# Two held-back products and a fixed start order in a chunked delta-rule attention feeding two gated layers

## Chip, core and metric

One core of one Trainium2 chip runs the whole program. The metric is the device time of one execution in microseconds (us), the median over several executions. The engines are TensorE (PE; PEld is its weight load), VectorE (DVE), ScalarE (ACT), GpSimd (POOL) and SyncE (SP), which issues the DMAs here.

## What is computed

```python
# attention, per batch b and head h (4 x 8), 768 steps, head size 48
k_n = k / (norm(k) + 1e-6)
for t in range(768):
    y[t] = q[t] @ state
    state = state + beta[t] * outer(k_n[t], v[t] - k_n[t] @ state)
x = y as [3072, 384]
# first layer, width 1536
x = (silu(x @ w_gate) * (x @ w_val)) @ w_out
# second layer, width 2048
x = elu(x @ w_in) @ w_out2
```

q, k, v and beta are float32. The weights arrive as float64, and the kernel turns each into a high and a low float32 part itself.

## The kernel before

The 3072 tokens are cut into 12 groups (NB) of 256, two batches by 128 steps each. For each group there is an attention part and a first-layer part; the second layer (512 tokens at a time, L506 to L538) runs behind all groups and the change doesn't touch it.

Attention of a group: `stage1` normalises k (`norm`, with a Sqrt on ACT), transposes q and k (`trans`, PE), and takes their products (`gram`, PE at L210). `inversion` then inverts a triangular matrix on DVE: four transposes (L227), some 116 small multiplies and adds (L248, L255) that each need the one before, and a transpose back (L263); ACT spreads the result into `zt` (L270). `xstep` (L281) applies it, `gstep` (L294, four rounds over four PSUM banks, copied out by ACT at L298 and completed by DVE at L299) builds the matrices of a step of 32, `chain` (L312) carries the state through them, `yall` (L325) gives y and `xtr` (L340) its transpose, split into `xh` and `xl`.

First layer of a group, for f = 0 to 11: `gv1` (L445) makes the gate and value products, 18 matmuls into one of two PSUM banks; ACT takes the Silu (L466), DVE multiplies (L467), ACT and DVE split the result into two parts of `hb` (L345, L348). `out1` (L479) multiplies `hb` with wo, 9 matmuls that add up in `acc` over all f; after f = 11 ACT copies `acc` out (L486) and SP stores it. `out1` comes LAG = 2 gate products behind its `gv1`. At the end of a group `moe1` empties the list `held`:

```python
while held:
    put(1, held.pop(0), 1.0, out1)
```

While the first layer of group g runs, attention of group g + 1 and the inversion for group g + 2 are merged into the same queues. `merge` orders the pieces by their weights, and each engine runs its queue in order.

Before the first gate product the 18 weight tiles must be loaded (SP, L363 and L366) and decoded in five pieces each: `low` (ACT, L389), `p0` (ACT, L396), `p1` (DVE, L404), `p2` (DVE, L409), and `p3`, a cast on ACT (L345) with a subtraction on POOL (L348). 16 tiles are loaded at the start, the last two when their room is free. Before, `anchor` and `pinned` only bind decode pieces behind the attention work that was emitted last on DVE and ACT, and a scheduler places the rest.

Of the kernel before, what the change touches and what calls it, by code (L numbers as in the profile page):

```python
# [21 lines left out]
def delta_moe_kernel(ctx: ExitStack, tc: tile.TileContext, q, k, v, beta,  # L22
# [9 lines left out]
    nc = tc.nc  # L32
# [30 lines left out]
    NTB = 2  # L63

# [40 lines left out]
    def emit_consts():  # L105
        make_identity(nc, ident)
        V.memset(neg1, -1.0)
# [13 lines left out]

    def emit_zero():
        V.memset(kp[:, :, D:64], 0.0)
        V.memset(qp[:, :, D:64], 0.0)
        G.memset(zt, 0.0)
        G.memset(st[0:32], 0.0)

        for r0, r1 in ((32, 64), (64, 96)):
            for x, n in ((st, B * H), (sv, 2 * (C - 1) * H)):
                w_ = x[r0:r1].rearrange("p b (h d) -> p b h d", d=D) if x is st else \  # L130
                    x[r0:r1].rearrange("p a c (h d) -> p (a c) h d", d=D)
                A.copy(out=w_.rearrange("p b h d -> p (b h) d"),
                       in_=ident[r0:r1, D:2 * D].unsqueeze(1).to_broadcast([32, n, D]))
# [61 lines left out]
    def trans(a, which):  # L195
# [23 lines left out]
    def inversion():  # L219
# [47 lines left out]
        def spread(r):  # L267
            def f():
                q0 = slice(32 * r, 32 * r + 32)
                A.copy(out=zt[q0, :, 32 * (r % 2):32 * (r % 2) + 32],  # L270
                       in_=ain[q0, 0:512].rearrange("p (u i) -> p u i", u=16))
# [4 lines left out]
    def xstep():  # L276
        for n in range(4):
# [6 lines left out]
            A.copy(out=R[:, 4 * n:4 * n + 4, :], in_=p)  # L284

    def gstep(a, par):
        b = 64 * par
        lc = buf['lc', a][par]
        ps_ = [nxt(atb, "at") for c in range(C)]
# [6 lines left out]
        for c in range(C):  # L296
            pv = ps_[c][0:96, 0:320].rearrange("p (s w) -> p s w", s=4)
            A.copy(out=lc[:, :, c, :], in_=pv)  # L298
# [22 lines left out]
    def yall(g, a):  # L321
# [7 lines left out]
        buf['y', a] = TT(f"y{a}", [128, DM])  # L329
        A.copy(out=buf['y', a], in_=p[:, 0:DM])  # L330
# [5 lines left out]
    def xtr(g, a):  # L336
        xs = slice(a * 128, a * 128 + 128)
        p = nxt(atb, "at")[:, 0:DM].rearrange("p (k t) -> p k t", k=KD)
        for kk in range(KD):
            nc.tensor.transpose(p[:, kk, :], buf['y', a][:, kk * 128:kk * 128 + 128], ident)  # L340
# [34 lines left out]
    def decode(n, tmps):  # L375
# [25 lines left out]
        def p1():  # L401
            if bits:
                by = buf[n].bitcast(U8).rearrange("p a (n b) -> p a n b", b=8)
                V.tensor_scalar(out=by[:, :, :, 3], in0=by[:, :, :, 7], scalar1=128, scalar2=None,  # L404
                                op0=ALU.bitwise_and)
# [67 lines left out]
    def out1(g, f):  # L473
# [9 lines left out]
        if f == F1 - 1:  # L483
            for d0, d1 in ((0, 2), (2, KD)):
                t = TT(f"hb{hb_slot()}", [128, d1 - d0, TB])
                A.copy(out=t, in_=acc[:, d0 // 2, 0:(d1 - d0) * TB].rearrange(  # L486
                    "p (d t) -> p d t", t=TB))
                nc.sync.dma_start(out=x2d[g, :, d0:d1, :], in_=t)
# [37 lines left out]
    def out2(n, f):  # L526
# [6 lines left out]
        if f == F2 - 1:  # L533
            for t in range(4):
                o = TT(("xh1", "xl1", "y0", "y1")[next(os2) % 4], [128, DM])
# [5 lines left out]
    def stage1(g):  # L541
        return [(0.4, lambda: (load_v(g, 0), load_v(g, 1), norm(g), nkn(g, 0), nkn(g, 1))),
                (1.0, lambda: (trans(0, 0), trans(1, 0))),
                (1.0, lambda: (kb(g, 0), kb(g, 1), trans(0, 1), trans(1, 1))),
# [9 lines left out]
    def attention(g, nx):  # L554
# [9 lines left out]
        s.append((2.9, xstep))  # L564
        s += [(1.3, lambda a=a, par=par: gstep(a, par)) for a in range(2) for par in range(2)]
# [13 lines left out]
        inv = inversion()  # L579
# [31 lines left out]
    def moe1(g, before, after):  # L611
# [16 lines left out]
        while held:  # L628
# [48 lines left out]
    ABS = 4  # L677
    PRE0 = 3

    def emit_all():  # L680
        load_k(0)
        emit_consts()
        emit_beta()
        load_q(0)
        for n in range(6):
# [3 lines left out]
        first = stage1(0)  # L689
        body, tail = attention(0, 1)  # L690
        for n in range(6, NW - 2):
            first.insert(1 + n - 6, (0, lambda n=n: load_w(n, src1(n))))
        inv = inversion()
        buf['dt'] = TT("dt", [128, 2, 2, DM], I32)
        dec = [decoding(n, ("xh1", 0, "xl1", 1)) for n in range(NW)]
        dec = [pinned(l) for l in dec]
        run(merge(anchor(first), sum(dec[:PRE0], [])))
        load_q(1)
        inv[0] = pinned([(0, inv[0])])[0][1]
        early = []  # L700
        for n in range(PRE0, PRE):
            early += dec[n][:2]
            del dec[n][:2]
        for n in range(PRE0, PRE0 + ABS):
            early.append(dec[n].pop(0))
        run(merge(anchor([(0.1, x) for x in inv]), anchor(early)))
        run(merge(anchor(body), sum(dec[PRE0:PRE], [])))
        for n in range(NW - 2, NW):
            load_w(n, src1(n))
        nd = [PRE]  # L710

        def before(n):
            l = []
            k = 0
            while nd[0] < NW and (nd[0] <= n or k < PACE):
                k += 1
                l += dec[nd[0]]
# [70 lines left out]
```

## Time and profile before

| | us |
|---|---|
| median of three executions | 1307.78 (1303.6 to 1320.31) |
| the profiled execution | 1302.85, span 1301.1 |
| PE busy | 1162.0 (89%) |
| DVE busy | 821.8 (63%) |
| ACT busy | 608.6 (47%) |
| POOL busy | 129.9 (10%) |

PE counts as busy from a matmul's start to its modelled end, so waits inside a run of matmuls can hide in it. Engines run their own queues in order; a row's square bracket tells how long the engine was idle before it and what ended that.

### The profile page before, as it was taken

Reading aid. Unit: us, or ns where it says so; the run is one execution under the profiler, and the core shown is the slowest. Engines: PE = TensorE matmul, PEld = TensorE weight load, DVE = VectorE, ACT = ScalarE, POOL = GpSimd, SP = SyncE. Lnnn points to the kernel's source line nnn. Section 1 sums busy time; section 2 is a strip of 40 time slices with the busy share of each in tenths; the row PEclk is TensorE's granted clock in tenths of the full one; section 3 lists DMA queues with packets and bytes.
Section 4 is the critical chain, followed back from the end, with each engine's and each line's share of the span. In section 5 each row is a group of like instructions: output and inputs, shape, how many; then the busy total and the mean of one; then the engine's idle time right before and its main releaser. Section 6 shows DMA issues by size and latency. Waiting matters only on the chain.

```text
span 1301.1 us, 31342 instructions
## 1 busy us (share of the span) xinstructions
PE 1162.0 (89%) x13086; PEld 1078.5 (83%) x13086; DVE 821.8 (63%) x2709; ACT 608.6 (47%) x1181; POOL 129.9 (10%) x106
## 2 busy tenths in 40 slices
PE   2473999898989898989898989989899999999998
PEld 1363889898888898989888989978689899899897
DVE  6799585848484858585848574467964545454443
ACT  7554534343425252535353524457754545454443
POOL 4353100000000000000000000031300000000000
PEclk9866798889999999999999999989999999999999
DMA  9530202020202020202020100373010101000000
GB/s 298 160 81 1 38 14 39 13 39 10 43 2 51 2 50 2 51 2 50 7 46 2 26 11 5 125 251 104 1 49 1 49 1 49 1 33 1 25 1 25
DMA packets 106815, 57.16 MB, mean 44 GB/s; under 512 B 76945, under 2 KB 101521, under 8 KB 106673
## 3 DMA queue, kind: packets, MB, share of 16 engines
q1 hardware_dynamic: 106672, 55.16, 16.7%
q8 instruction: 102, 1.67, 0.5%
q14 instruction: 41, 0.33, 0.1%
HBM read 45.71 MB, written 9.44 MB: 42 GB/s over the span
## 4 chain that ended last, share of the span: by engine, by line
PE 57%; DVE 34%; ACT 4%; issue 3%; DMA 1%; POOL 1%; SPq 0%; DVEq 0%; ACTq 0%; POOLq 0%
PE gv L445 14%; DVE z L255 7%; DVE ain L248 7%; PE acc L531 7%; PE at L531 7%; PE at L514 7%; PE gv L514 7%; PE acc L479 5%; PE at L294 4%; DVE w L404 2%; PE at L281 2%; DVE hb L348 2%; DVE tb L467 2%; DVE ain L227 2%; PE at L312 2%
## 5 line engine op out<-in xcount | busy, mean ns | idle before, releaser
L445 PE MATMUL gv<-xh,w 128*128 128x256 f32 x1728 | 295.9, 295 | 23.6 <-DVE tb L467 22.9
L445 PEld LDWEIGHTS gv<-xh,w 128*128 128x128 f32 x1728 | 248.9, 200 | 29.4 <-DVE tb L467 24.0
L479 PE MATMUL acc<-hb,w 128*128 128x256 f32 x1296 | 194.9, 298 | 37.6 <-ACT hb L345 34.7
L479 PEld LDWEIGHTS acc<-hb,w 128*128 128x128 f32 x1296 | 172.2, 199 | 45.5 <-ACT hb L345 36.7
L445 PE MATMUL gv<-xl,w 128*128 128x256 f32 x864 | 160.6, 295 | 1.5 <-DVE xl L348 1.5
L466 ACT ACTIVATE tb<-gv 128x256 f32<-128x256 f32 x144 | 54.9, 382 | 216.4 <-PE gv L445 216.0
L467 DVE TENSOR_TENSOR tb<-gv,tb 128x256 f32<-128x256 f32 x144 | 60.7, 422 | 127.6 <-ACT tb L466 126.7
L445 PEld LDWEIGHTS gv<-xl,w 128*128 128x128 f32 x864 | 131.7, 202 | 2.9 <-DVE xl L348 1.7
L345 ACT CAST hb<-tb 128x256 fp32r<-128x256 f32 x144 | 58.4, 406 | 146.8 <-DVE tb L467 146.2
L255 DVE TENSOR_TENSOR z<-z,ain 128x60 f32<-128x60 f32 (+32 forms) x696 | 122.5, 214 | 1.3
L248 DVE TENSOR_TENSOR ain<-z,ain 128x60 f32<-128x60 f32 (+32 forms) x696 | 122.3, 207 | 1.2
L348 DVE TENSOR_TENSOR hb<-tb,hb 128x256 fp32r<-128x256 f32 x144 | 76.7, 533 | 42.7 <-ACT hb L345 41.3
L521 DVE SCALAR_TENSOR_TENSOR hb<-at,hb 128x512 f32<-128x512 f32 x48 | 33.2, 691 | 84.5 <-ACT hb L520 84.5
L521 DVE SCALAR_TENSOR_TENSOR hb<-gv,hb 128x512 f32<-128x512 f32 x48 | 33.1, 690 | 80.2 <-ACT hb L520 72.5
L294 PE MATMUL at<-gr,R 32*96 32x80 f32 x1536 | 75.3, 276 | 8.7 <-DVE w L299 4.4
L294 PEld LDWEIGHTS at<-gr,R 32*96 32x96 f32 x1536 | 64.9, 179 | 19.0 <-DVE w L299 4.6
L520 ACT ACTIVATE hb<-hb,neg 128x512 f32<-128x512 f32 x96 | 69.4, 723 | 2.8
L518 ACT ACTIVATE hb<-at 128x512 f32<-128x512 f32 x48 | 28.6, 595 | 87.6 <-PE at L514 87.6
L518 ACT ACTIVATE hb<-gv 128x512 f32<-128x512 f32 x48 | 28.6, 596 | 85.3 <-PE gv L514 85.0
L281 PE MATMUL at<-R,zt 64*64 64x96 f32 x768 | 38.6, 254 | 27.5 <-ACT zt L270 27.4
L519 ACT ACTIVATE hb<-hb 128x512 f32<-128x512 f32 x96 | 60.6, 632 | 2.7
L281 PEld LDWEIGHTS at<-R,zt 64*64 64x64 f32 x768 | 35.8, 140 | 29.7 <-ACT zt L270 28.2
(174 smaller groups left out, 2154.6 us busy)
## 6 DMA issues: line engine op xcount, KB each, us to landing
w<-in_moe_w_out_dram SPq DMA_DIRECT2D x28, 384.0 KB, 6.6
w<-in_moe_w_in_dram SPq DMA_DIRECT2D x16, 384.0 KB, 5.6
kp<-in_k_dram SPq DMA_DIRECT2D x12, 384.0 KB, 5.4
qp<-in_q_dram SPq DMA_DIRECT2D x12, 384.0 KB, 4.3
w<-in_moe_w_gate_dram SPq DMA_DIRECT2D x12, 384.0 KB, 7.8
w<-in_moe_w_val_dram SPq DMA_DIRECT2D x12, 384.0 KB, 8.0
R<-in_v_dram SPq DMA_DIRECT2D x24, 192.0 KB, 2.6
x2d<-hb SPq DMA_DIRECT2D x12, 256.0 KB, 2.1
```

The lines of the kernel that those rows point to most:

```text
L248: V.tensor_tensor(out=t, in0=z[:, l:l + 1, x:y].to_broadcast([128, l, y - x]), in1=an[:, l, 0:l].unsqueeze(2).to_broadcast([128, l, y - x] ...
L255: V.tensor_tensor(out=z[:, 0:l, x:y], in0=z[:, 0:l, x:y], in1=t, op=ALU.add)
L281: nc.tensor.matmul(p[r:r + 64, j], lhsT=zt[r:r + 64, 4 * n + j, :], rhs=R[r:r + 64, 4 * n + j, :], start=True, stop=True, skip_group_check ...
L294: nc.tensor.matmul(ps_[c][0:96, s * 80:s * 80 + 80], lhsT=R[t, u, :], rhs=gr[t, u, 0:80], start=True, stop=True, skip_group_check=True)
L348: (e2 or V).tensor_tensor(out=lo, in0=src, in1=hi.bitcast(F32), op=ALU.subtract)
L445: nc.tensor.matmul(dst, lhsT=wt[:, a_, kk * 128:(kk + 1) * 128], rhs=xx[:, kk, :], start=(n == 0), stop=(n == 3 * KD - 1))
L467: V.tensor_tensor(out=s, in0=p[:, TB:2 * TB], in1=s, op=ALU.mult)
L479: nc.tensor.matmul(o, lhsT=w[:, a_, d * 128:(d + 1) * 128], rhs=hh[:, b_, :], start=(f == 0 and n == 0 and d != 1), stop=(f == F1 - 1 and ...
L514: nc.tensor.matmul(p, lhsT=W[f][:, 0, a_, kk * 128:(kk + 1) * 128], rhs=x2[n][b_][:, kk, :], start=(m == 0), stop=(m == 3 * KD - 1))
L520: A.activation(out=r, in_=r, func=ACTF.Identity, bias=neg1, scale=1.0)
L521: V.scalar_tensor_tensor(out=r, in0=p, scalar=0.0, in1=r, op0=ALU.max, op1=ALU.add)
L531: nc.tensor.matmul(ob4[t], lhsT=hh[:, b_, t * 128:(t + 1) * 128], rhs=w[:, a_, :], start=(f == 0 and m == 0), stop=(f == F2 - 1 and m == 2))
```

## The change

Three things change.

First, `held` is emptied at a group's end only in the last group. The last two wo products of a group (f = 10 and 11) come behind the first two gate products of the next one. The copy of `acc` no longer goes to an `hb` tile but to one tile `y`, which the two halves of the attention's y now share.

Second, everything up to the first gate product is emitted by `inorder`, which binds each piece behind the one before it on DVE, ACT and POOL: attention of group 0 first, then the inversion together with all `low` pieces, then the attention's remainder merged with the decode of nine tiles (NE; before it was 13, PRE). All 16 weight tiles are issued before v. A Sqrt on one element stands first on ACT.

Third, copies change engines: those that fill `st` and `sv` go from ACT to POOL, behind `kb`, as part of `emit_zero2`; and in group 0 alone ten evacuations (two of `kq`, two of `zt`, two of `R`, four of `lc`) go from ACT to DVE. There `gstep` also uses the four banks of `gv` and `acc` in turn with the four `at` banks.

```diff
+    def emit_zero2():
         G.memset(zt, 0.0)
         G.memset(st[0:32], 0.0)
...
-                A.copy(out=w_.rearrange("p b h d -> p (b h) d"),
-                       in_=ident[r0:r1, D:2 * D].unsqueeze(1).to_broadcast([32, n, D]))
+                G.tensor_copy(x[r0:r1], ident[r0:r1, D:2 * D].unsqueeze(1).to_broadcast([32, n, D]))
...
+    def put(out_, p, on_v):
+        (V.tensor_copy if on_v else A.copy)(out=out_, in_=p)
...
-        A.copy(out=kq[:, a, :, which, :], in_=p)
+        put(kq[:, a, :, which, :], p, g == 0 and a)
...
+        if g == 0 and (a + par) % 2 == 0:
+            ps_ = gvb + [acc[:, 0], acc[:, 1]]
+        else:
+            ps_ = [nxt(atb, "at") for c in range(C)]
...
-        while held:
+        while held and g == NB - 1:
             put(1, held.pop(0), 1.0, out1)
...
-        for n in range(6):
+        for n in range(2):
+            load_w(n, src1(n))
+        for n in range(2, NW - 2):
             load_w(n, src1(n))
...
+        norm_, tq, tk, gm = stage1(0)
+        run(inorder([norm_, tq, piece(0, 0), tk, gm, (0, emit_zero2)]))
+        early = [piece(n, i) for n in range(4) for i in (0, 1)][1:]
+        early += [piece(n, 0) for n in range(4, NW - 2)]
+        inv = inversion(0)
+        run(inorder(merge([(0.1, x) for x in inv[:-4]], early)))
...
+        run(inorder([(0, x) for x in inv[-4:]]))
+        run(inorder(merge(body, pre)))
```

Line numbers of the changed kernel run some 3 to 15 higher: L445 is now L460, L479 L494, L281 L287, L294 L303, L227 L233, L263 L269, L404 L419, L409 L424; `put` is L199, for both engines.

PE at the end of a group in the middle of the program, before. The last gate product of the group (f = 11, bank gv_84) is followed by the wo products of f = 9 and 10 and, behind one matmul of the next group, that of f = 11:

```order
L445 MATMUL gv_84<-xh_140_3448,w_59_1047 128x256 x3
L445 MATMUL gv_84<-xl_141_3449,w_59_1047 128x256 x3
L445 MATMUL gv_84<-xh_140_3448,w_59_1047 128x256 x6
L479 MATMUL acc<-hb_182_4637,w_53_926 128x256 x9
L479 MATMUL acc<-hb_184_4694,w_60_1086 128x256 x9
L445 MATMUL gv_83<-xh_172_4379,w_21_203 128x256
L479 MATMUL acc<-hb_186_4749,w_60_1086 128x256 x9
L445 MATMUL gv_83<-xh_172_4379,w_21_203 128x256 x2
```

The same place in the changed kernel:

```order
L460 MATMUL gv_84<-xh_133_3420,w_62_1157 128x256 x3
L494 MATMUL acc<-hb_174_4638,w_55_1035 128x256 x9
L460 MATMUL gv_83<-xh_163_4349,w_26_436 128x256 x3
L460 MATMUL gv_83<-xl_164_4350,w_26_436 128x256 x3
L494 MATMUL acc<-hb_176_4709,w_63_1188 128x256 x9
L287 MATMUL at_87<-R,zt 64x96 x8
L287 MATMUL at_88<-R,zt 64x96 x8
```

A whole gate product of the next group now stands between the wo products of f = 9 and f = 10; the one of f = 11 has moved behind `xstep` and a second gate product. `xstep` stands one gate product earlier than before.

POOL at the start of the program, before (z is the mask of `norm`, later the inversion's tile; w are decoded weights):

```order
L126 MEMSET st 32x1536
L177 TENSOR_TENSOR z_153<-strict,nbt 128x512
L192 TENSOR_TENSOR gr<-kp,nbt 128x8x48 x2
L348 TENSOR_TENSOR w_21_203<-xh_20_189,w_21_203 128x2x384
L348 TENSOR_TENSOR w_22_222<-dt_140,w_22_222 128x2x384
L230 MEMSET z_307 128x512
```

and in the changed kernel:

```order
L180 TENSOR_TENSOR z_177<-strict,nbt 128x512
L195 TENSOR_TENSOR gr<-kp,nbt 128x8x48 x2
L130 MEMSET zt 128x1024
L131 MEMSET st 32x1536
L136 COPY st<-ident 32x1536
L136 COPY sv<-ident 32x2304
L136 COPY st<-ident 32x1536
L136 COPY sv<-ident 32x2304
L236 MEMSET z_286 128x512
```

Two fills and four copies now stand ahead of the MEMSET of z that the inversion starts from, and two subtractions of the decode behind it.

DVE behind the first inversion, before (its last transpose, then decode pieces of tiles 3 to 5, then `gstep`):

```order
L263 STREAM_TRANSPOSE ain<-z_307 128x32x16
L404 TENSOR_SCALAR w_5_116<-w_5_116 128x768
L404 TENSOR_SCALAR w_6_119<-w_6_119 128x768
L409 SCALAR_TENSOR_TENSOR dt_140<-dt_140,w_5_116 128x768
L409 SCALAR_TENSOR_TENSOR xh_26_424<-xh_26_424,w_6_119 128x768
L404 TENSOR_SCALAR w_7_122<-w_7_122 128x768
L299 TENSOR_TENSOR lc_446<-at_87,kq 48x4x32
```

and in the changed kernel:

```order
L269 STREAM_TRANSPOSE ain<-z_286 128x32x16
L199 COPY zt<-ain 32x16x32 x2
L419 TENSOR_SCALAR w_2_108<-w_2_108 128x768
L424 SCALAR_TENSOR_TENSOR xh_20_282<-xh_20_282,w_2_108 128x768
L199 COPY R<-at_88 128x384
L199 COPY R<-at_86 128x384
L419 TENSOR_SCALAR w_3_111<-w_3_111 128x768
L424 SCALAR_TENSOR_TENSOR dt_165<-dt_165,w_3_111 128x768
```

One tile's pieces (tile 0) now stand between the inversion and the first copy of `R`, which needs `xstep` on PE; ahead of the inversion no decode piece is left on DVE, where three of `p1` and three of `p2` stood.

## Rows read from the trace of the kernel before

**Rows 1.** PE's waits, 190 to 880 us: total us, times, longest.
```profile
PE acc L479 <- ACT hb L345: 33.5, 9, 4.1
```
**Rows 2.** Timeline of one group: start, us, engine, line, [idle before, releaser].
```profile
486.14 1.34 PE L479 MATMUL acc<-hb,w 128*128 128x256 f32 x9
487.41 2.22 DVE L227 STREAM_TRANSPOSE ain<-gr 128x256 f32<-128x256 f32 x4
...
500.62 0.52 PE L445 MATMUL gv<-xh,w 128*128 128x256 f32 x3
502.78 1.24 PE L479 MATMUL acc<-hb,w 128*128 128x256 f32 x9
...
509.99 2.66 PE L479 MATMUL acc<-hb,w 128*128 128x256 f32 x18
512.30 1.08 DVE L263 STREAM_TRANSPOSE ain<-z 128x512 f32<-128x512 f32 x1
513.46 1.25 ACT L270 COPY zt<-ain 32x512 f32<-32x512 f32 x2 [2.42 <-DVE ain L263]
516.46 1.47 POOL L166 TENSOR_TENSOR ain<-kp 128x768 f32<-128x768 f32 x1 [1.89 <-ACT zt L270]
516.86 2.41 PE L479 MATMUL acc<-hb,w 128*128 128x256 f32 x9 [4.10 <-ACT hb L345]
518.13 0.94 DVE L167 TENSOR_REDUCE sm<-ain 128x16 f32<-128x768 f32 x1
521.72 1.28 ACT L466 ACT_TABLE_LOAD   x1
523.94 2.86 PE L281 MATMUL at<-R,zt 64*64 64x96 f32 x64
524.86 0.48 ACT L284 COPY R<-at 128x384 f32<-128x384 f32 x1
...
552.09 1.19 DVE L227 STREAM_TRANSPOSE ain<-gr 128x256 f32<-128x256 f32 x2
```
**Rows 3.** Windows: busy us (x) of PE, PEld, DVE, ACT, POOL; granted clock; DMA.
```profile
141.00:156.00 15.00, 15.00 (x153) 13.51 (x153) 6.41 (x21) 9.15 (x21) 1.66 (x2) 0.54 0.19 38
516.00:521.00 5.00, 4.14 (x21) 4.03 (x22) 2.23 (x2) 2.46 (x5) 1.47 (x1) 0.66 0.05 17
```
**Rows 4.** Timeline, end of group 0.
```profile
185.50 1.34 PE L479 MATMUL acc<-hb,w 128*128 128x256 f32 x9 [1.18 <-ACT hb L345]
```
**Rows 5.** Windows over the start, columns as in rows 3 (last: DMA GB/s).
```profile
0.00:46.80 46.80, 7.46 (x150) 6.34 (x150) 36.34 (x150) 33.19 (x39) 15.61 (x21) 1.00 1.06 306
10.00:44.00 34.00, 4.80 (x137) 4.06 (x136) 30.65 (x140) 22.60 (x30) 10.05 (x7) 1.00 1.08 354
46.80:60.00 13.20, 10.79 (x126) 9.86 (x127) 6.15 (x11) 7.29 (x17) 5.60 (x3) 0.85 0.18 27
0.00:132.40 132.40, 58.89 (x864) 53.04 (x865) 112.62 (x356) 76.08 (x113) 52.67 (x40) 0.78 0.48 133
```
**Rows 6.** Timeline of the start, ACT, POOL and DVE.
```profile
3.25 1.37 POOL L126 MEMSET st<- 32x1536 f32 x1
12.83 0.18 DVE L170 TENSOR_SCALAR sm<-sm 128x16 f32<-128x16 f32 x1 [4.91 <-ACT sm L168]
14.89 2.57 POOL L192 TENSOR_TENSOR gr<-kp,nbt 128x384 f32<-128x384 f32 x2 [4.05 <-DVE kp L184]
...
28.13 0.19 DVE L248 TENSOR_TENSOR ain<-z,ain 128x31 f32<-128x31 f32 x1
43.68 1.06 DVE L263 STREAM_TRANSPOSE ain<-z 128x512 f32<-128x512 f32 x1
46.20 1.88 ACT L270 COPY zt<-ain 32x512 f32<-32x512 f32 x3
...
131.24 1.16 DVE L263 STREAM_TRANSPOSE ain<-z 128x512 f32<-128x512 f32 x1
```

**Rows 7.** DVE's groups of instructions, 0 to 132 us: busy us, mean ns, idle before.
```profile
L404 DVE TENSOR_SCALAR w<-w 128x768 uint8<-128x768 uint8 x18 | 24.9, 1418 | 1.1 <-ACT w L389 1.1
```

More of the change, by code (lines that the diff above doesn't have):

```diff
@@ L283, in xstep, with gstep @@
                                      skip_group_check=True)
-            A.copy(out=R[:, 4 * n:4 * n + 4, :], in_=p)
-    def gstep(a, par):
+            put(R[:, 4 * n:4 * n + 4, :], p, g == 0 and n % 2)
+    def gstep(g, a, par):
         b = 64 * par
         lc = buf['lc', a][par]
-        ps_ = [nxt(atb, "at") for c in range(C)]
+        if g == 0 and (a + par) % 2 == 0:
+            ps_ = gvb + [acc[:, 0], acc[:, 1]]
+        else:
+            ps_ = [nxt(atb, "at") for c in range(C)]
         for s in range(4):
@@ L297, in gstep @@
             pv = ps_[c][0:96, 0:320].rearrange("p (s w) -> p s w", s=4)
[L298 removed]
+            put(lc[:, :, c, :], pv, g == 0 and c == 3)
             V.tensor_tensor(out=lc[0:D, :, c, D:80], in0=pv[0:D, :, D:80],
@@ L563, in attention @@
             s.append((0, lambda: load_k(nx)))
-        s.append((2.9, xstep))
-        s += [(1.3, lambda a=a, par=par: gstep(a, par)) for a in range(2) for par in range(2)]
+        s.append((2.9, lambda: xstep(g)))
+        s += [(1.3, lambda a=a, par=par: gstep(g, a, par)) for a in range(2) for par in range(2)]
         def ch(c):
@@ L675, in pinned, with inorder, wrap, f @@
         return [(w, wrap(x)) for w, x in l]
-    ABS = 4
-    PRE0 = 3
+    def inorder(l):
+        def wrap(x):
+            def f():
+                with ExitStack() as es:
+                    for e in (mybir.EngineType.DVE, mybir.EngineType.Activation,
+                              mybir.EngineType.Pool):
+                        if e in last:
+                            es.enter_context(tc.issue_after(last[e]))
+                    n = len(traced())
+                    x()
+                    for i in traced()[n:]:
+                        last[i.engine] = i
+            return f
+        return [(w, wrap(x)) for w, x in l]
+    NE = 9
     def emit_all():
         load_k(0)
+        emit_beta()
         emit_consts()
-        emit_beta()
         load_q(0)
-        for n in range(6):
+        for n in range(2):
+            load_w(n, src1(n))
+        for n in range(2, NW - 2):
             load_w(n, src1(n))
@@ L688, in emit_all, with piece @@
         emit_beta2()
-        first = stage1(0)
-        body, tail = attention(0, 1)
[L691 to L707, printed above, removed]
+        buf['dt'] = TT("dt", [128, 2, 2, DM], I32)
+        tmps = ("xh1", 0, "xl1", 1)
+        dec = [decode(n, tmps) if n < NW - 2 else None for n in range(NW)]
+        def piece(n, i, w=WD):
+            return (w, lambda: dec[n][i]())
+        norm_, tq, tk, gm = stage1(0)
[4 more added lines that the diff above has]
+        run(inorder(merge([(0.1, x) for x in inv[:-4]], early)))
+        load_q(1)
+        body, tail = attention(0, 1)
+        pre = []
+        for n in range(NE):
+            pre += [piece(n, 2), piece(n, 3), piece(n, 4)]
+            if n + 4 < NE + 2:
+                pre.append(piece(n + 4, 1))
+        run(inorder([(0, x) for x in inv[-4:]]))
+        run(inorder(merge(body, pre)))
+        late_ = []
+        for n in range(NE, NW - 2):
+            late_.append([piece(n, i) for i in ((2, 3, 4) if n < NE + 2 else (1, 2, 3, 4))])
         for n in range(NW - 2, NW):
             load_w(n, src1(n))
-        nd = [PRE]
+        nd = [NE]
         def before(n):
```

51 lines of the change are left out of this document (29 added, 22 removed).

## The prediction

> **What bounds the kernel now.** I began with the table of engines: PE is busy 89% of the span, DVE 63%. So I asked PE's waits first, over the stretch of the twelve groups. One line carries nearly all: the wo product waits for the cast of `hb`, 33.5 us in 9 waits [rows 1].
>
> The timeline of one such place shows what is late. DVE ends the inversion's last transpose at 513.4; ACT then makes two spreads of `zt` ahead of the Silu of f = 11, because that is its queue order, then two more, and only then the cast of `hb`. PE stands idle for 4.10 us [rows 2]. The nine matmuls behind the wait take 2.41 us, double pace, and the granted clock from 516 to 521 is 0.66, a mix of the lower and the higher level [rows 3]. So a boundary costs PE 4.1 us of idling and, as 0.34 of 5 us, another 1.7 us of half clock.
>
> The same rows give the loop that sets the period. From L227 at 487.41 to the next L227 at 552.09 are 64.7 us [rows 2]: 26.0 us of inversion on DVE to 513.4, 10.5 us until `xstep` starts at 523.94, and 28.15 us of PE work from there to the next transposes. Only the middle piece holds a wait.
>
> The start is different. DVE's idle time until the end of the second inversion (132.4) is 132.4 - 112.6 = 19.8 us [rows 5]; from 60 us on it is almost never idle, and PE waits for it. There DVE is the bound.
>
> **The boundary, step by step.** PE's order between the end of `gram` and `xstep` grows by one gate product and loses one wo product. Before, PE went from 486.14 to 509.99 without a long wait and had done six gate and six wo products and the attention's pieces [rows 2]. The changed order adds one of each ahead of the next group's first gate product. A gate product takes 502.78 - 500.62 = 2.16 us; a wo product about 1.1 (half of the 2.41 at half clock is 1.2, less a little for the overlap with the next matmul). So PE comes to that gate product at 486.14 + 23.85 + 3.3 = 513.3. It needs the bank of f = 10, whose multiply stands on DVE just behind the last transpose: 513.4 + 0.4 for it = 513.9. A wait of 0.6 us. The gate product ends at 516.1, the wo product of f = 10 at 517.2. By then `zt` is spread (516.4, where POOL's next work starts, rows 2). So `xstep` starts at 517.2 instead of 523.94: 6.7 us earlier [rows 2].
>
> Then three differences until the next transposes. One wo product more: 1.1. A new wait: ACT does the Silu and cast of f = 11, two table loads around the Sqrt (1.28 each), and the Sqrt waits for POOL (1.47) and DVE (0.94) behind the spreads; Silu of the next gate product and four copies of `R` (0.48 each) come to about 523.1 [rows 2], while PE, done with `xstep` (2.86) and a gate product, wants the copies at 522.2. Wait 0.9. On the other side the four `gstep` rounds now each have a full product between them; before, two neighbours stood with four matmuls between, and I credit 0.8 for that. Sum: 28.15 + 1.1 + 0.9 - 0.8 = 29.35, so the next L227 comes at 546.6 and the period is 59.2: **5.5 us per boundary**, if the clock stays up.
>
> Will it? After the 1.18 us wait at the end of group 0 nine matmuls took 1.34 us, full pace [rows 4], so a wait of 0.6 or 0.9 by itself need not drop it. The bounds are 5.5 (no drop) and 5.5 - 2 x 1.7 = 2.1 (a drop at each of the two waits). I take 4.7, nearer to the first because of that row. Nine boundaries have a wait: 9 x 4.7 = 42. The mean wait is 33.5 / 9 = 3.7, not 4.1, so 9 x 0.4 = 3.6 of that was never there to win: **-39 us**. Group 0's end loses its 1.18 us: **-1**.
>
> The copy of `acc` moves between two `gstep` copies on ACT. It must be done before the wo product f = 0 of the next group, behind a whole gate product and a `gstep` round (over 3 us) for two copies of 0.9 us together, so I cost it at nothing; without that cover it would be up to 0.9 per group. The shared `y` tile is stored some 30 us before the attention writes it again: nothing.
>
> **The start, step by step.** The Sqrt is no longer behind ACT's copies: of DVE's wait of 4.91 us [rows 6] some 4.6 go, and `kb` on POOL starts at 10.3 instead of 14.89 and ends at 12.9. But POOL then does two fills (1.37, rows 6, and by its elements 0.9) and four copies of 1536 or 2304 elements, 7,680 in sum, before the MEMSET of z (0.5) that the inversion needs. The trace has no copy on POOL. Lower bound, the fill's 1.37/1536 = 0.89 ns an element: 6.8 us. Upper bound, the two-input multiply's 1.47/768 = 1.91 ns [rows 2]: 14.7 us. One input is nearer to the fill than to two; I take 9. So the inversion starts at 12.9 + 2.3 + 9 + 0.5 = 24.7 (22.5 to 30.4) instead of 28.13, and with the same 16.6 us (28.13 to 44.74, rows 6) ends at 41.3 (39.1 to 47.0).
>
> The Trainium skill, GPSIMD Engine Reference, section "Elementwise — side-by-side cycle accounting", gives POOL about 1.8 cycles of 1.2 GHz an element at best in a software loop. By that the copies would take an estimated 11.5 us and the inversion end at 43.8, which is 2.5 us above my value and still hidden by what follows. No run so far shows such a copy.
>
> It is hidden because `xstep` also needs v, and v is now issued behind all 16 weight tiles. The bytes ahead of it are those that had landed by about 44 us before: 10 to 44 us moved 354 GB/s without a break [rows 5], 12.0 MB after some 1.8 MB, and 16 tiles of 786 KB with k, q, beta and v are 13.9 MB. So v lands at about 44. ACT's spreads stand behind the `low` of the last tile, which lands one v earlier (0.39 MB, 1.1 us), so at 43.8, plus two spreads of 0.63: 45. Before, the fourth spread ended at 48.1 [rows 6]. `xstep` gains 3 us, and loses up to 1 in POOL's slow case (47.0 plus two spreads on DVE is 48.3).
>
> That gain doesn't count, since DVE is the bound and now starves. Of its 36.3 us of work until 46.8 [rows 5] eight decode pieces are part, and six of these move behind `xstep`: 6 x 1.4 [rows 7] = 8.5 us. Four of the ten copies taken over from ACT come in, 2.3 us. So 30.1 us of work by the time when the first copy of `R` can go (45 plus two of four blocks, about 47), and 17 us idle. What is left is the rest of the same 112.6 us plus all ten copies, 4.7 us by ACT's 0.4 to 0.6 each. Idle time behind it was 7.05 us from 46.8 to 60 [rows 5]; now a tile's two pieces, the norm's reduction and the larger choice of PSUM banks fill part of it, and I take 4. Sum: 112.6 + 4.7 + 17 + 4 = 138.3 against 132.4: **+6 us**. Bounds: 0 later idle and no cost of the copies, -3; POOL's slow case and 7 us of idle, +12. What PE has done by the second `xstep` is the same in both orders, so the loss is passed on whole.
>
> **Sum.** 1302.85 (the profiled execution, 5 us below the median of the runs shown) + 6 - 1 - 39 = **1269 us**.
>
> **The rivals.** *The clock falls at the new waits.* Each boundary has two short waits around products of small tiles. For it: 141 to 156 us ran at 0.54 with PE busy throughout [rows 3]. Against: rows 4. Price: 2.1 a boundary, less the 0.4 of above, 15 in all: 1302.85 + 6 - 1 - 15 = 1293.
>
> *DVE doesn't starve at the start, and the boundaries win in full.* For it: much of DVE's time at the start is contended and may shrink. Then 0 for the start and 9 x 5.1 = 46: 1256.
>
> *Slower: `xstep` and `gstep` fall to half clock in every group.* As said, 141 to 156 us, exactly these products, had 0.54 without idling: 15 x 0.46 = 6.9 us lost. If moving `xstep` next to the boundary's waits brings this into nine more groups, 62 us are lost: 1269 + 62 = 1331. It decides from 4.7 us lost a group on. Against: in the group of rows 2 the same products ran at full pace.
>
> *It doesn't do what it says.* The loop through DVE could hold `xstep` where it was: if DVE's 26 us stretch by the 5 us that PE runs ahead, the wait only moves. For it: DVE is busy throughout those 26 us. Against: the same pieces stand there, five multiplies and splits, in both orders. Then only the half clock goes, 9 x 1.7: 1302.85 + 6 - 15 = 1294, as the first rival.
>
> **Chances.** Forecast 0.55 (1258 to 1280); clock or loop 0.25 (1280 to 1297); full gain 0.14 (1246 to 1258); slower 0.06. The range for 8 in 10 runs from 1249 to 1293. Two per cent, about what a measurement of this kernel can tell, is 26 us: faster takes the full gain, nine tenths of the forecast and a little of the third, 0.65; within 2% 0.30; slower 0.05.
>
> **What would show it.** In the changed profile L494's wait for `hb` should be under 5 us in all, the period from L233 to L233 near 59 us, and the granted clock near 1.00 behind the boundaries. At the start the first `xstep` should stand near 45 and the second inversion's end near 138; DVE should be idle some 10 us before the first copy of `R`. It would be wrong if L287 or L460 waits over 2 us a group, or if clock rows near 0.5 follow `xstep`.

## The result, and the profile after the change

| | before | changed |
|---|---|---|
| median of three executions, us | 1307.78 | 1257.83 (1252.91 to 1258.09) |
| ratio, 95% interval | 1 | 0.959 (0.948 to 0.969) |
| profiled execution, us | 1302.85, span 1301.1 | 1258.09, span 1256.3 |

The ratio comes from interleaved executions of both kernels. A longer comparison further down gives 0.963 (0.960 to 0.967). The kernel is faster by 4%, and the time lies inside the range of the prediction, 11 us below its single number. Two terms of the sum were too small, the gain at the boundaries and the loss at the start, and they pulled in opposite directions.

First, PE's waits in the stretch of the groups, the view of [rows 1] (waiting line and releaser: us, times, longest):

```profile
PE gv L460 <- DVE tb L482: 4.3, 2, 3.0
PE gv L460 <- ACT xh L355: 4.0, 1, 4.0
PE acc L494 <- ACT y L501: 1.7, 1, 1.7
PE at L216 <- issue: 1.6, 1, 1.6
```

The wait for the cast of `hb` (33.5 us in nine times before) no longer appears. What is left are single events: one at the end of group 0 (for `xh`), one at 408 us (issue), the others behind the last `xstep`.

The timeline of one boundary, to be held against [rows 2] (start, us, engine, line; the square bracket is the idle time before):

```profile
471.25 2.21 DVE L233 STREAM_TRANSPOSE ain<-gr 128x256 f32<-128x256 f32 x4
...
496.22 1.16 DVE L269 STREAM_TRANSPOSE ain<-z 128x512 f32<-128x512 f32 x1
497.23 0.41 DVE L482 TENSOR_TENSOR tb<-gv,tb 128x256 f32<-128x256 f32 x1
497.47 0.62 ACT L199 COPY zt<-ain 32x512 f32<-32x512 f32 x1 [3.23 <-DVE ain L269]
497.69 0.62 PE L460 MATMUL gv<-xh,w 128*128 128x256 f32 x3
498.42 1.89 ACT L199 COPY zt<-ain 32x512 f32<-32x512 f32 x3
499.95 1.24 PE L494 MATMUL acc<-hb,w 128*128 128x256 f32 x9
501.12 1.12 PE L287 MATMUL at<-R,zt 64*64 64x96 f32 x21
...
529.68 2.21 DVE L233 STREAM_TRANSPOSE ain<-gr 128x256 f32<-128x256 f32 x4
```

The multiply on DVE that frees the bank of f = 10 ends at 497.64, and PE starts the gate product that needs it at 497.69. The last spread ends at 500.31, `xstep` starts at 501.12. PE has work at every moment: it comes to this gate product 0.05 us behind the multiply, and to `xstep` 0.8 us behind the spread.

Then one period, from `xstep` to `xstep`, in windows (busy us and instructions of PE, PEld, DVE, ACT, POOL; granted clock; DMA share, GB/s). The first row is of the kernel before, the second of the changed one:

```profile
523.94:588.68 64.74, 60.14 (x923) 56.92 (x922) 44.09 (x195) 26.63 (x63) 4.70 (x5) 0.97 0.15 27
```
```profile
501.12:559.55 58.43, 58.43 (x923) 55.53 (x923) 42.74 (x194) 26.31 (x63) 4.71 (x6) 1.00 0.17 29
```

The same 923 matmuls. Before, PE idled 4.60 us of the period and worked at 0.97 of its clock, 60.14 x 0.03 = 1.8 us; together 6.4, and the period is shorter by 6.31. Now PE is busy for the whole period at the full 2.4 GHz. So at this boundary, as far as the profile shows it, nothing more is to be had by waiting less.

The start, in windows as in [rows 5], and the timeline of its starving stretch:

```profile
0.00:49.25 49.25, 9.73 (x190) 8.82 (x191) 30.50 (x149) 23.69 (x32) 17.23 (x23) 0.65 1.06 298
0.00:142.60 142.60, 56.23 (x864) 51.36 (x865) 119.57 (x366) 64.58 (x99) 54.51 (x44) 0.66 0.45 123
```
```profile
38.04 1.08 DVE L269 STREAM_TRANSPOSE ain<-z 128x512 f32<-128x512 f32 x1
41.92 0.96 DVE L424 SCALAR_TENSOR_TENSOR xh<-xh,w 128x768 int32<-128x768 int32 x1
44.30 0.90 ACT L399 ACTIVATE w<-w 128x768 int32<-128x768 uint32 x1 [1.43 <-DMA w<-in_moe_w_val_dram]
45.10 1.24 ACT L199 COPY zt<-ain 32x512 f32<-32x512 f32 x2
49.25 0.56 DVE L199 COPY R<-at 128x384 f32<-128x384 f32 x1 [6.37 <-PE at L287]
141.42 1.17 DVE L269 STREAM_TRANSPOSE ain<-z 128x512 f32<-128x512 f32 x1
```

The first inversion ends 5.6 us earlier than before (38.04 against 43.68 in [rows 6]). ACT's spreads stand behind the `low` of the last tile, at 44.30, and DVE has nothing to do from 42.9 to 49.25. The second inversion's last transpose comes at 141.42 instead of 131.24: 10.2 us late.

**Where the time went.** The start of each `xstep` on PE, read from the two timelines, divides the difference of the spans:

| stretch | before, us | changed, us | gain, us |
|---|---|---|---|
| start to second `xstep` | 133.73 | 143.92 | -10.2 |
| second to third | 59.12 | 59.34 | -0.2 |
| third to the last (nine periods) | 592.46 | 536.56 | +55.9 |
| last `xstep` to the end | 515.79 | 516.48 | -0.7 |
| sum (the spans) | 1301.1 | 1256.3 | +44.8 |

The nine periods gave 6.2 each on average; five of them are between 57.9 and 58.5 us. One, from 380 to 443 us, took 62.92: PE idled 2.6 us in it for "issue", a wait that the profile ascribes to no other engine, and lost 1.7 us to half clock. Such a period, of 61.6 to 65.2 us, stands at the same place in the kernels below that share these groups, so it decides nothing between them; what it comes from stays open.

### The profile page after: what moved, and what is told of

The parts are those of the page before. It is cut to its first block, busy times and chain, and to the rows that moved or that the text cites. A ratio compares the mean times of both kernels' runs of the same rounds, so it can differ in the third digit from the quotient of the medians.

```text
span 1256.3 us, 31338 instructions
## 1 busy us (share of the span) xinstructions
PE 1142.3 (91%) x13086; PEld 1061.5 (84%) x13086; DVE 819.1 (65%) x2719; ACT 596.8 (48%) x1167; POOL 131.7 (10%) x110
## 4 chain that ended last, share of the span: by engine, by line
PE 78%; DVE 10%; DMA 4%; issue 3%; ACT 2%; POOL 1%; SPq 1%; DVEq 0%; POOLq 0%; ACTq 0%
PE gv L460 23%; PE acc L494 11%; PE acc L546 7%; PE at L546 7%; PE at L529 7%; PE gv L529 7%; PE at L303 5%; PE at L321 3%; PE at L287 3%; DVE w L419 2%; PE at L206 2%; PE at L334 1%; DVE ain L254 1%; PE at L216 1%; DVE z L261 1%
## 5 line engine op out<-in xcount | busy, mean ns | idle before, releaser
L460 PE MATMUL gv<-xh,w 128*128 128x256 f32 x1728 | 295.1, 294 | 38.0 <-DVE tb L482 32.8
L460 PEld LDWEIGHTS gv<-xh,w 128*128 128x128 f32 x1728 | 245.1, 197 | 43.6 <-DVE tb L482 33.8
L494 PE MATMUL acc<-hb,w 128*128 128x256 f32 x1296 | 185.5, 288 | 2.3 <-ACT y L501 1.7
L494 PEld LDWEIGHTS acc<-hb,w 128*128 128x128 f32 x1296 | 165.9, 192 | 5.9 <-ACT y L501 1.9
L460 PE MATMUL gv<-xl,w 128*128 128x256 f32 x864 | 155.9, 290 | 0.2 <-issue 0.2
L460 PEld LDWEIGHTS gv<-xl,w 128*128 128x128 f32 x864 | 128.8, 198 | 1.9 <-issue 1.6
L254 DVE TENSOR_TENSOR ain<-z,ain 128x60 f32<-128x60 f32 (+32 forms) x696 | 125.8, 212 | 1.6
L355 ACT CAST hb<-tb 128x256 fp32r<-128x256 f32 x144 | 58.5, 407 | 142.8 <-DVE tb L482 142.7
L358 DVE TENSOR_TENSOR hb<-tb,hb 128x256 fp32r<-128x256 f32 x144 | 68.6, 477 | 29.2 <-ACT hb L355 28.9
L303 PE MATMUL at<-gr,R 32*96 32x80 f32 x1472 | 71.4, 264 | 1.2 <-DVE lc L308 1.2
L533 ACT ACTIVATE hb<-at 128x512 f32<-128x512 f32 x48 | 28.7, 597 | 87.4 <-PE at L529 87.4
L303 PEld LDWEIGHTS at<-gr,R 32*96 32x96 f32 x1472 | 58.5, 167 | 13.5 <-DVE lc L308 2.0
L533 ACT ACTIVATE hb<-gv 128x512 f32<-128x512 f32 x48 | 28.7, 597 | 84.8 <-PE gv L529 84.8
L287 PE MATMUL at<-R,zt 64*64 64x96 f32 x768 | 37.2, 251 | 31.4 <-ACT zt L199 31.4
L287 PEld LDWEIGHTS at<-R,zt 64*64 64x64 f32 x768 | 34.7, 137 | 33.3 <-ACT zt L199 31.8
```

The costliest lines, as they stand in the source:

```text
L254: V.tensor_tensor(out=t, in0=z[:, l:l + 1, x:y].to_broadcast([128, l, y - x]), in1=an[:, l, 0:l].unsqueeze(2).to_broadcast([128, l, y - x] ...
L287: nc.tensor.matmul(p[r:r + 64, j], lhsT=zt[r:r + 64, 4 * n + j, :], rhs=R[r:r + 64, 4 * n + j, :], start=True, stop=True, skip_group_check ...
L303: nc.tensor.matmul(ps_[c][0:96, s * 80:s * 80 + 80], lhsT=R[t, u, :], rhs=gr[t, u, 0:80], start=True, stop=True, skip_group_check=True)
L358: (e2 or V).tensor_tensor(out=lo, in0=src, in1=hi.bitcast(F32), op=ALU.subtract)
L460: nc.tensor.matmul(dst, lhsT=wt[:, a_, kk * 128:(kk + 1) * 128], rhs=xx[:, kk, :], start=(n == 0), stop=(n == 3 * KD - 1))
L494: nc.tensor.matmul(o, lhsT=w[:, a_, d * 128:(d + 1) * 128], rhs=hh[:, b_, :], start=(f == 0 and n == 0 and d != 1), stop=(f == F1 - 1 and ...
```

## The experiments

**The held products alone.** The kernel before with nothing but this, and the `y` tile that it needs:

```diff
-        while held:
+        while held and g == NB - 1:
```

> The kernel before with the first part of the change alone: the last two wo products of a group are held back into the next, and the copy of acc goes to the shared y tile; the start is that of before. Theory A (the boundary gives back all of its idling and all of its half clock, and the new start costs what its second xstep is late): second xstep at 133.7 us as before, period of a group 58.5 us, no wait of the wo product for hb, and 1302.85 - 55.7 (what the changed kernel gained between its second and its last xstep) = about 1247 us. Rival B (a part of those 55.7 us came from the new start: the half-clock stretches of before at 203-210, 271-278 and 339-343 us cost 8.5 us and are gone or shorter in the changed kernel): those stretches stand in this run too, 1247 + 8.5 = about 1256 us.

Measured: 1246.13 us, 0.955 of before (0.951 to 0.959). The second `xstep` starts at 134.05, six of the nine periods from the third on are between 57.9 and 58.7 us, and there is no wait for `hb`. PE's waits from the second to the last `xstep`:

```profile
PE gv L446 <- ACT xh L346: 2.9, 1, 2.9
PE at L312 <- issue: 2.1, 2, 1.7
PE at L210 <- issue: 1.7, 1, 1.7
```

Theory A holds, to within a microsecond. Rival B falls: of the half-clock stretches 203-210, 271-278 and 339-343 none is left in its place, with the old start. They belonged to the boundaries too, although they stood 17 to 19 us behind the end of a boundary wait, and 10 to 11 us behind an `xstep`. This kernel is faster than both others.

**The new start alone.** The changed kernel with `while held:` again.

> The changed kernel with the list of held products emptied at each group's end again, so only the new start and the moved copies are left. Theory A: second xstep at 143.9 us as in the changed kernel, 10.2 later than before, then boundaries as before with 4.1 us of waiting for hb and a period of 64.7 us: 1302.85 + 10.2 = about 1313 us. Rival (the late start is given back later, because the first groups have slack while the last weight tiles are decoded): 1303 to 1306 us.

Measured: 1311.82 us, 1.0058 of before (1.003 to 1.009), that is 7.6 us slower, second `xstep` at 144.26. The waits of PE from 190 to 880 us are back (this profiled execution took 1319.4 us, above its median, so I read nothing finer from it):

```profile
PE acc L494 <- ACT hb L355: 36.6, 10, 4.1
```

So the start costs 8 to 10 us with either kind of boundary, and it isn't given back later.

**DVE's empty stretch filled.** The two DVE pieces of tiles 1 to 3 go ahead of the first copy of `R`:

```diff
+        gap = [piece(n, i) for n in range(4) for i in (2, 3)]
         for n in range(NE):
-            pre += [piece(n, 2), piece(n, 3), piece(n, 4)]
+            pre += ([] if n < 4 else [piece(n, 2), piece(n, 3)]) + [piece(n, 4)]
...
         run(inorder([(0, x) for x in inv[-4:]]))
+        run(inorder(gap))
```

> The changed kernel with the two decode pieces on DVE of tiles 1 to 3 bound ahead of the first copy of R, where DVE was idle for 6.4 us, instead of behind it. Theory A (DVE's idle time at the first xstep is what makes the start late): second xstep 6.3 us earlier (three times 2.1), at 137.6, and about 1252 us. Rival (the casts on ACT and the subtractions on POOL of these tiles come earlier too and collide with the copies of R and lc, so the work is only contended elsewhere): second xstep within 2 us of 143.9, 1256 to 1258 us.

Measured: second `xstep` at 139.44, 1249.46 us. 4.5 of the 6.3 us arrived. The rest can be seen behind the gap, in DVE's timeline:

```profile
47.72 2.23 DVE L424 SCALAR_TENSOR_TENSOR dt<-dt,w 128x768 int32<-128x768 int32 x1
49.87 0.55 DVE L199 COPY R<-at 128x384 f32<-128x384 f32 x1
54.88 0.95 DVE L170 TENSOR_REDUCE sm<-ain 128x16 f32<-128x768 f32 x1 [3.54 <-POOL ain L169]
```

DVE doesn't wait for `R` any more, but 3.5 us for POOL, where the decode's subtractions now stand earlier, ahead of the square for the next norm. The idle stretch is the cause of somewhat less than half of the loss (4.5 of 10.2 us), and filling it makes a smaller wait elsewhere.

**What holds the first `xstep`.** `low` of tiles 13 to 15 behind the spreads; and then v early as well, in which `stage1` no longer issues v for group 0:

```diff
-        early += [piece(n, 0) for n in range(4, NW - 2)]
+        early += [piece(n, 0) for n in range(4, NW - 5)]
...
+            if n < 3:
+                pre.append(piece(NW - 5 + n, 0))
```

```diff
-        for n in range(2, NW - 2):
+        for n in range(2, 6):
+            load_w(n, src1(n))
+        load_v(0, 0)
+        load_v(0, 1)
+        for n in range(6, NW - 2):
             load_w(n, src1(n))
```

> The changed kernel with the low pieces of tiles 13 to 15 behind the spreads of zt on ACT instead of ahead; v is still issued behind all 16 weight tiles. Theory A (the last low piece is what holds the spreads, and v would have landed soon behind the last tile, at 43 to 44 us): first xstep at 43 to 44 instead of 45.8. Rival (v itself ends the wait): first xstep within 0.5 us of 45.8. In both cases the second xstep gains no more than 2.5 us: 141.4 to 143.9, and the time is 1255 to 1258 us.

> As the run with low behind the spreads, and v issued behind 6 weight tiles instead of 16. Theory A (with both out of the way the inversion, which ends at 39.1, is what xstep waits for): first xstep at 41 us, 4.8 earlier; DVE starves that much less and the second xstep comes at 139, the time is about 1253 us. Rival (the decode on DVE is bound by what is decoded later, not by the idle stretch): first xstep at 41, but second xstep still above 142.

Measured: with `low` later the first `xstep` starts at 44.76, released by v:

```profile
44.76 5.47 PE L287 MATMUL at<-R,zt 64*64 64x96 f32 x64 [29.12 <-DMA R<-in_v_dram]
```

That is 0.8 us behind the bound of theory A and 1.0 ahead of the changed kernel: the two waits lie one behind the other, within a microsecond, `low` last. With v early too it starts at 42.23 and not at 41: one `low`, at 40.77, again stands ahead of ACT's spreads. The second `xstep` comes at 140.76 (`low`) and 140.16 (both), the time is 1252.85 and 1254.07. The first run gained 3.2 us at the second `xstep` for 1.0 at the first, more than either theory gave it; the second gained 3.8 of the expected 4.9. So the second `xstep` follows the first only loosely. My reading, which no run here tries by itself, is that it counts what DVE has to do and not when one piece starts.

**The ten copies on ACT again.**

```diff
-        (V.tensor_copy if on_v else A.copy)(out=out_, in_=p)
+        A.copy(out=out_, in_=p)
```

> The changed kernel with the ten copies of group 0 on ACT again. Theory A (DVE bounds the start, and the copies are 6.0 us of its work: kq 1.4, zt 1.6, R 1.1, lc and w 1.9; those of kq and zt, 3.0, lie where DVE waits anyway): second xstep 3 us earlier than 143.9, at 141, time about 1255 us. Rival (ACT's queue then makes DVE wait for lc as in the kernel before, 5.1 us at 50 us): second xstep at 144 or later, time 1258 to 1260 us.

Measured: second `xstep` at 145.27, 1254.68 us. DVE's waits up to there:

```profile
DVE sm L170 <- POOL ain L169: 8.3, 1, 8.3
DVE gr L219 <- ACT xh L406: 4.1, 1, 4.1
DVE w L308 <- ACT w L199: 4.0, 2, 3.5
```

The rival is right at the start: what DVE no longer does, it now waits for. How far the second `xstep` can be trusted is shown by five profiles with the same start (the changed kernel twice, the start alone and the last two variants below): they have it at 143.2 to 144.3, so differences of about 1 us say nothing. The single time is 3 us lower than the changed kernel's median although its second `xstep` comes later; the changed kernel's own executions reach from 1252.3 to 1258.2, so from such single times I read nothing, and judge the start by the second `xstep`.

**The fills first on POOL.**

```diff
-        run(inorder([norm_, tq, piece(0, 0), tk, gm, (0, emit_zero2)]))
+        run(inorder([(0, emit_zero2), norm_, tq, piece(0, 0), tk, gm]))
```

> The changed kernel with the fills of zt and st and the four copies to st and sv first on POOL, from about 2 us on, instead of behind kb. Theory A (the first xstep waits for v and the last low piece, not for the inversion): the inversion starts at 17.5 instead of 22.3 and ends at 34.5 instead of 39.1, but the first xstep stays at 45.8, DVE only waits 4.8 us longer for it, and the time stays at 1258 us. Rival (an earlier inversion is an earlier xstep): first xstep at 41, second at 139, 1253 us.

Measured: the inversion starts at 23.4 and not at 17.5, first `xstep` at 45.34, second at 144.70, 1253.91 us. My own premise failed. The rows of DVE and POOL beside each other show why:

```profile
6.05 2.83 POOL L136 COPY sv<-ident 32x2304 f32<-32x2304 f32 x1
8.92 1.46 POOL L136 COPY st<-ident 32x1536 f32<-32x1536 f32 x1
10.33 2.10 POOL L136 COPY sv<-ident 32x2304 f32<-32x2304 f32 x1
...
7.08 1.83 DVE L121 COPY zd<-sm 128x16 f32<-128x16 f32 x1
8.95 1.47 DVE L122 TENSOR_SCALAR zd<-zd 128x16 f32<-128x16 f32 x1
10.32 0.94 DVE L170 TENSOR_REDUCE sm<-ain 128x16 f32<-128x768 f32 x1
```

The same two instructions of the changed kernel, with POOL waiting at that time:

```profile
6.52 0.17 DVE L121 COPY zd<-sm 128x16 f32<-128x16 f32 x1
6.73 0.18 DVE L122 TENSOR_SCALAR zd<-zd 128x16 f32<-128x16 f32 x1
```

0.17 us became 1.83, 0.18 became 1.47: each of the two ends within 0.05 us of the end of the copy that POOL does beside it (at 8.88 and 10.38). The norm's reduction starts 3.5 us later than in the changed kernel and the inversion's first transposes 6.1 later (21.33 against 15.27), more than the 4.8 us of waiting that went away. The question that the run was for (is the first `xstep` held by the inversion?) is answered by the run with v early instead: it comes 3.5 us sooner there behind an inversion that ends at the same time, so no.

**All four of the start together.** v early, `low` of six tiles behind the spreads, fills first, copies on ACT.

> The changed kernel with four edits of the start together: v issued behind 6 tiles, the low pieces of tiles 10 to 15 behind the spreads, the fills of st and sv first on POOL, and the ten copies on ACT. Theory A (the start is bound by DVE's work plus its idle time: 119.6 - 6.0 of work, 12.3 - 4.8 of idling ahead of the inversion and 4.3 behind the first xstep): first xstep at about 36, second at 125 to 128, the time 1258 - 17 = about 1241 us. Rival (DVE waits for data or ACT again, since ACT has the copies and the decode): second xstep at 134 or later, 1248 us or more.

Measured: first `xstep` at 41.73, second at 141.23, 1253.67 us. DVE's waits:

```profile
DVE lc L308 <- ACT lc L199: 6.2, 3, 4.7
DVE gr L219 <- ACT xh L406: 4.1, 1, 4.1
```

The rival holds. The edits don't add: each takes away a wait that another one puts back.

**The held products and the fills on POOL, with the old start.** The run with the held products alone, and its four copies on POOL:

```diff
-                A.copy(out=w_.rearrange("p b h d -> p (b h) d"),
-                       in_=ident[r0:r1, D:2 * D].unsqueeze(1).to_broadcast([32, n, D]))
+                G.tensor_copy(x[r0:r1], ident[r0:r1, D:2 * D].unsqueeze(1).to_broadcast([32, n, D]))
```

> The kernel before with the held products (as the first run) and one more edit: the four copies that fill st and sv on POOL, behind its own fills, instead of on ACT; the scheduler's order of the start stays. Theory A (DVE's 5.1 us of waiting for the first Sqrt, which stands behind these copies on ACT, move the whole start): the inversion starts at 23 instead of 28 us, second xstep at 129 instead of 134.05, and 1246 - 5 = about 1241 us. Rival (what is won ahead of the inversion is lost behind it, where the first xstep waits for the spreads behind low pieces and DVE for lc): second xstep within 1 us of 134, 1245 to 1247 us.

Measured: 1246.66 us, 0.9575 (0.952 to 0.963), second `xstep` at 133.47: the rival again, no difference to 1246.13. Theory A fails at its first step: the inversion starts at 28.7 and not at 23. DVE's wait for the Sqrt falls from 5.1 to 1.6 us, but the same two short instructions take 1.83 and 1.47 us, and DVE is busy for 115.30 us until the second `xstep` instead of 112.29.

**A longer inversion.** The last transpose is made three times from group 2 on, the same values again:

```diff
-        lst.append(back)
+        lst.append((lambda: (back(), back(), back())) if g > 1 else back)
```

> The changed kernel with the inversion's last transpose done three times instead of once from group 2 on (the same values again): 2 x 1.16 = 2.3 us more on DVE ahead of the spreads. In the changed kernel xstep starts 0.8 us behind the last spread. Theory A (no more slack than these 0.8 us, and the clock stays up behind a short wait): PE waits 1.5 us for zt in each of ten groups, the period goes from 58.5 to 60.0, the time from 1258 to about 1273 us. Rival B (each such wait costs the clock too, as the waits of 2.5 to 4.1 us of the kernel before did with 1.7 us each): period 61.6, about 1289 us. Rival C (PE has other work that hides it): period 58.5, 1258 us.

Measured: 1275.76 us, 18 more. One of its periods, and PE's rows at the boundary one period earlier:

```profile
568.28:628.78 60.50, 58.41 (x923) 55.40 (x923) 45.36 (x195) 26.23 (x64) 4.70 (x5) 1.00 0.16 29
```
```profile
507.81 0.38 PE L287 MATMUL at<-R,zt 64*64 64x96 f32 x2 [0.20 <-ACT zt L199]
509.49 2.69 PE L287 MATMUL at<-R,zt 64*64 64x96 f32 x60 [1.29 <-ACT zt L199]
```

0.20 + 1.29 = 1.49 us of waiting for `zt`, exactly the 2.3 - 0.8 of theory A, and another 0.6 behind it in this period, where `gstep` waits for DVE. The full 1.49 us stands at six of the boundaries. The clock stayed at 1.00 in this period, but not everywhere: from 220 to 760 us there are four stretches of half clock, 1.7 us each. One, at 630, begins at a new wait, two, at 272 and 333, some 10 us behind one, and one, at 416, behind the "issue" wait that the changed kernel has too. Theory A holds for the wait, and C falls. B falls as a rule, but half clock follows three of the six waits, two of them at a distance, so the 18 us are more than the waits alone.

**One product held instead of two.**

```diff
-        while held and g == NB - 1:
+        while held and (g == NB - 1 or len(held) > 1):
```

> The changed kernel with only the last wo product (f = 11) held back into the next group and that of f = 10 again ahead of the boundary. Theory A (the wait came from the product of f = 11 alone, and that of f = 10 needs little time more than it has: its hb is split at 498.9 in the changed kernel where PE would come at 497.7): a wait of 1.2 us a group, period 59.6, about 1269 us. Rival B (f = 10 in its old place holds up PE by more, since PE comes to the boundary sooner without the stall): a wait of 2 us or more with half clock behind it, period 62 or more, 1290 us and up. Rival C (one held product does it all): period 58.5, 1258 us.

Measured: 1274.86 us, period about 61.0. One period, and the waits of 200 to 760 us:

```profile
449.03:510.07 61.04, 59.07 (x924) 55.98 (x923) 43.87 (x194) 26.48 (x64) 4.70 (x5) 1.00 0.14 28
```
```profile
PE gv L460 <- DVE tb L482: 6.0, 7, 0.9
PE at L303 <- DVE lc L308: 4.5, 9, 0.5
PE at L303 <- ACT R L199: 3.1, 7, 0.5
```

None of the three theories has the mechanism. The product of f = 10 doesn't wait in its old place. PE comes to the next gate product 0.9 us too early, then to `gstep` 0.5 us ahead of the copies of `R` and 0.5 ahead of DVE: three short waits, 61.04 - 59.07 = 2.0 us a period at full clock (and 0.6 more of modelled busy time). Two other periods have a stretch of half clock (332 to 336 and 517 to 520 us) and are 62.5 long. About 3.7 of the 6.3 us are won by the first held product and 2.6 by the second.

**The changed kernel again.**

> The changed kernel again, in more rounds, to set it against the run with the held products alone (0.955 of before). Theory A (the new start costs the 10 us by which its second xstep is late): 0.955 + 10/1304 = 0.963 of before, second xstep again at 143.9. Rival (the two kernels take the same time, since the late start is given back in the groups): 0.955, within 0.003.

Measured: 1256.75 us, 0.963 (0.960 to 0.967), second `xstep` at 144.08. It lies just clear of the 0.955 (0.951 to 0.959) of the held products alone. Theory A holds: with the start of before the kernel takes about 10 us less.

## Why the prediction came out as it did

**The boundary: mechanism right, size too small.** I had 39 us for nine boundaries; they gave 55.9, as the run with the held products alone shows too. `xstep` 29.8 us behind the inversion's first transposes was forecast and it starts at 501.12 - 471.25 = 29.87. The step is right, its exactness partly luck: PE came to the gate product 0.55 us later than forecast, which took the place of a wait of 0.6 that I had put there. Three terms failed:

- The new waits of 0.6 and 0.9 us. The estimate put PE at the gate product 0.6 us ahead of DVE and at the copies of `R` 0.9 ahead of ACT. Neither happened: 0.05 us lie between the multiply's end and the gate product. With 28.56 us from `xstep` to the next transposes instead of 29.35, the period is 58.43 instead of 59.2, which is 7 us over nine periods. The waits appear, with nearly these sizes (0.9, 0.5, 0.5), in the run with one held product: I had the right suspects and the wrong amount of work in between.
- The clock. I took 4.7 of 5.5 us to allow for drops at those waits, another 7 us over nine periods. There were no waits to drop at. That such waits would have left the clock alone isn't shown: in the kernel with a longer inversion half clock followed three of six.
- Stretches left out of the sum. What a boundary costs stands in one row that I didn't use: the whole period in one window, 4.60 us of idling and 0.97 of the clock, 6.4 us, as above. I had priced one wait and the half clock right behind it, and missed the second stretches of half clock behind the first three boundaries, 203 to 210 us and its like, 8.5 us in all. Instead I subtracted 3.6 us for shorter waits.

Nine times the 6.31 us of one period are 56.8. The early and the last periods of the kernel before were longer than 64.74, by 9.8 us in sum, and the four long periods of the changed kernel, of 60.1 to 62.9 us, take 10.7 back: 55.9. That these two nearly cancel is luck; neither was in the forecast.

The copy of `acc`, which I cost at nothing, has no wait behind it in the nine periods, and one of 1.7 us behind the last `xstep`.

**The end of group 0: -1 forecast, +0.2 measured.** PE no longer waits 1.18 us for `hb` there. It waits 4.0 for `xh` at the next gate product instead. The prediction had no such step, though the kernel before shows the wait already, 1.51 us behind the one for `hb`:

```profile
189.06 0.62 PE L445 MATMUL gv<-xl,w 128*128 128x256 f32 x3 [1.51 <-DVE xl L348]
```

With the held products and the old start the wait for `xh` is 2.9 and 3.5 us in two kernels, so most of it doesn't come from the late start. In a second profile of the changed kernel this period is 57.14 us instead of 59.34, with less half clock in it, so the +0.2 itself isn't firm.

**The start: direction right, 10.2 instead of 6.** The first `xstep` at 45 (45.76), the starving of DVE (17 us forecast; 49.25 - 30.50 = 18.75, of which 6.37 right before the first copy of `R`) and later idling of 4 (4.3) were nearly right. The first `xstep` gained 1.1 us and not 3: the 48.1 that I compared with is the end of the fourth spread, and before, `xstep` started at 46.87, behind the second. Right was the range for the copy on POOL, 2.10 us for 2304 elements and 1.46 for 1536, near the lower bound, so that the inversion began at the early bound of 22.5. By the Trainium skill's best case for an unrolled loop (GPSIMD Engine Reference, "Elementwise — side-by-side cycle accounting") I had an estimated 11.5 us for the four copies; they took 7.1, and the rows decide.

Two terms were too small. The work: I kept 112.6 us and added 4.7 for ten copies, and DVE did 119.57, 2.3 more. The copies themselves are 6.0 (kq 1.4, zt 1.6, R 1.1, lc and w 1.9); all other work together grew by 0.95. The idling: 23.0 us instead of 21, nearly all of the difference ahead of the first copy of `R`. Together 4.3, and 138.3 + 4.3 is the 142.6 at which the second inversion ends.

That the other work grew by so little hides two changes that nearly cancel. Ahead of the second inversion it became shorter: `p1` took 21.8 us in all instead of 24.9, as my second rival had expected of contended work. Inside the second inversion it became longer. The second inversion, from its first transposes to its last, took 29.3 us before (from 101.91) and 41.8 now (from 99.58: up to here the changed kernel was ahead, by 2.3 us). DVE's instructions in this stretch, first of before, then of the changed kernel:

```profile
L255 DVE TENSOR_TENSOR z<-z,ain 128x60 f32<-128x60 f32 (+32 forms) x58 | 13.6, 267 | 0.1
L248 DVE TENSOR_TENSOR ain<-z,ain 128x60 f32<-128x60 f32 (+32 forms) x58 | 11.9, 234 | 0.1
L404 DVE TENSOR_SCALAR w<-w 128x768 uint8<-128x768 uint8 x3 | 3.1, 1035 | 0.0
L348 DVE TENSOR_TENSOR hb<-tb,hb 128x256 fp32r<-128x256 f32 x4 | 1.7, 416 | 0.0
```
```profile
L254 DVE TENSOR_TENSOR ain<-z,ain 128x60 f32<-128x60 f32 (+32 forms) x58 | 15.1, 291 | 0.1
L261 DVE TENSOR_TENSOR z<-z,ain 128x60 f32<-128x60 f32 (+32 forms) x58 | 13.5, 263 | 0.1
L419 DVE TENSOR_SCALAR w<-w 128x768 uint8<-128x768 uint8 x6 | 6.2, 1038 | 0.0
L358 DVE TENSOR_TENSOR hb<-tb,hb 128x256 fp32r<-128x256 f32 x4 | 3.1, 786 | 0.1
```

Thirteen decode pieces of `p1` and `p2` lie here instead of six, 7.1 of the 12.5 us, and eight subtractions on POOL instead of four: the inversion's own multiplies and adds grow from 25.5 to 28.6 us, the four splits of `hb` from 1.7 to 3.1. The decode was moved out of a stretch where DVE waited into one where DVE is the bound. That the contention with POOL is what stretches those multiplies is read from rows such as the 0.17 and 1.83 us above and was not tried in this stretch by itself.

**The rivals.** The falling clock, the loop through DVE (1293, 1294) and the half clock in every group (1331) did not come: the inversion takes 26.1 us in the changed kernel, and the granted clock is 1.00 over whole periods. Full gain at the boundaries came, and with it the loss at the start, a pair that none of my cases had. The 1257.83 falls, by 0.2 us, in the bracket of the case in which DVE doesn't starve; that case's mechanism did not come. That the sum missed by only 11 us is in part luck: 17 us too little at the boundaries against 4 too little at the start, and 2 lost at group 0's end and behind the last `xstep`.

## What to carry to other kernels

Price a recurring stall by one whole period, idle time plus busy time times the missing share of the clock, and not by the wait that is named: here 6.4 us against 4.1, or 5.8 with the half clock right behind it. When a change has two halves, read them apart: the held products alone gave 0.955, both 0.963. Before moving work out of the way, look for who is idle where it stood and who is the bound where it goes, and expect an order on three engines to answer one removed wait with another.

## What the runs showed of the hardware

Two short DVE instructions beside copies on POOL lasted until the copy ended: 0.17 us became 1.83 and 0.18 became 1.47, in two kernels to the hundredth. The 0.94 us reduction behind them ran beside the next copy at its usual length, so it isn't every instruction. And in the kernel before, the granted clock of PE fell to half at or behind eight of the nine boundary waits of 2.5 to 4.1 us; with a longer inversion, half clock followed three of six waits of 0.2 and 1.3 us.
